# Narrowing the second half of the first expert's output weights in that expert's first two tiles

## The chip, the core and the metric

The kernel runs on one core of one Trainium2 chip. The metric is the device time of one execution in microseconds (us); of several executions the median counts.

## The reference

Four batches of talking-heads attention (12 heads, 448 positions, head size 64) are followed by two dense experts over 1792 tokens of width 768.

```python
scores = einsum(scale * q @ k.T, w_pre)          # mixes heads
attn = einsum(softmax(scores), w_post)           # mixes heads again
x = (attn @ v) laid out as 1792 x 768

h = x @ w_in                                     # first expert, 768 -> 1024
solu = h * softmax(h)
x = (normalised(solu) * g_ln) @ w_out            # 1024 -> 768

g = relu(x @ w2_in) ** 2                         # second expert, 768 -> 2048
out = g @ w2_out                                 # 2048 -> 768
```

The weights of both experts arrive as 64-bit words (the launch hands their arrays over as int64 views). The kernel has to make 32-bit floats of them itself; this is what "narrowing" means below.

## The kernel before, in words

The program's order is written by hand: each engine executes its instructions in the order in which the Python code emits them, and a function that yields lets the caller place its steps between other work.

**Attention.** The loop at line 624 goes over slots. A slot takes two blocks of ten query rows through the head mixing before the softmax (`pre`), row maxima (`negmax`, line 267), exponentials (`expo`, line 274), weights (`weigh`, line 285 and 287, once a slot), the head mixing after it (`post`, line 307) and the copy out of PSUM (`post_out`, line 337). Some slots also hold score matmuls (`qk`) or value matmuls (`av`, line 373). A last `x_out` (line 403) stores the attention's result as xD.

**Narrowing the first expert's weights** happens in the slots of the attention. `w1pieces` (line 413) lists pieces of 128 x 256 words: 24 of w_in, then 24 of w_out. `load_w1` (line 419) loads one through POOL's queue. `narrow` needs a square on ACT (line 82) and three operations on DVE (lines 85, 89, 93) that put the 32-bit word together; `flush` (lines 102 and 103) sets tiny numbers to zero in two operations on POOL; `scale_w1` (line 440) multiplies a piece of w_out by g_ln on ACT; `store_w1` (line 445) writes it back to HBM through SP's queue. Lines 618 to 645 pace the loads: `share` is the traffic of a slot if all pieces and the other loads are spread evenly over slots 5 to 63. The DVE steps are put in by `filler`, seven in each slot that has an `av` (line 675).

**First expert.** The loop at line 919 goes over 14 tiles `m` of 128 tokens. It loads and splits tile m + 2 into a high and a low part (`load_x`, `split_x`: ACT line 762, POOL line 763), runs the matmuls `h1` of tile m (line 500), then `norm1` (lines 773 to 794: the row maximum on DVE, exp on ACT, the product, statistics and their aggregate on DVE, rs on POOL, nb on DVE, the scaling on ACT), then `zt` of tile m - 1 (transposes on PE, line 809, a cast on ACT and a subtraction on DVE, line 812). The weights of w_out are loaded and split two blocks of 128 rows a tile in tiles 0 to 3 (`load_w1_out`, `split_w1_out`: ACT line 748, POOL line 749). From tile 4 on, two output matmul groups `out1` (line 823) stand in each tile.

**Narrowing the second expert's weights** is done by `w2stream` (line 844), which is stepped with `steps2`. A piece is loaded through SP (line 852), squared on ACT (line 862), made a mask on POOL (line 863: one operation), put together by three operations on DVE (lines 887, 891, 893) that take the mask in, and stored through SP (line 870). A load waits for the buffer of the piece five before it. `rate` says how many steps stand at each of four places in a tile:

```python
def rate(m, n):
    return 0 if m <= GT else n if m < NTILE - 1 else n // 2
...
steps2(rate(m, 4))
next(norm)
```

With GT = 3 no step stands in tiles 0 to 3; from tile 4 on there are 4 + 6 + 4 + 4 = 18 steps a tile. Sixty pieces go there, 36 later, in the second expert (line 1324), whose loop over 16 passes ends the program.

Of the kernel before, what the change touches and what calls it, by code (L numbers as in the profile page):

```python
# [11 lines left out]
AF = mybir.ActivationFunctionType  # L12
# [6 lines left out]
def kernel(  # L19
# [16 lines left out]
    nc = tc.nc  # L36
# [3 lines left out]
    NT, DM = out.shape  # L40
    F1 = w1_in.shape[1]
# [13 lines left out]
    scale = 1.0 / float(D) ** 0.5  # L55
# [7 lines left out]
    w1oD = dram.tile([F1, DM], F32, name="w1oD")  # L63
# [11 lines left out]
    g_sb = const.tile([128, F1 // 128], F32, name="g_sb")  # L75
# [64 lines left out]
    for b in range(B):  # L140
        for (i0, n) in CHUNKS:
# [10 lines left out]
            elif odd:  # L152
                k = nks[0] - 1
                order = [(1, k)] + order[:-2] + [(0, k)]
            for h, k in order:
                r = len(range(k, (n0, n - n0)[h], nks[h]))
# [9 lines left out]
    kk = {}  # L166
# [241 lines left out]
    WP = 256  # L408
# [2 lines left out]
    w1s = {}  # L411
    w1t = {}
    w1pieces = [(w1_in, w1iD, k, o) for k in range(CC) for o in range(0, F1, WP)]
    w1pieces += [(w1_out, w1oD, k, o) for k in range(F1 // 128) for o in range(0, DM, WP)]

    def load_w1(i):
        src, dst, k, o = w1pieces[i]
# [92 lines left out]
    def run(part):  # L510
        for _ in part:
            pass
# [215 lines left out]
    K1 = F1 // 128  # L728
# [16 lines left out]

    def split_w1_out(kk, r):
        t = m1_p.tile([128, 2, DM], F32R, name=f"w1o{kk}")
        nc.scalar.copy(t[:, 0], r)
        nc.gpsimd.tensor_tensor(out=t[:, 1], in0=r, in1=t[:, 0].bitcast(F32), op=ALU.subtract)  # L749
        w1o.append(t)  # L750
# [46 lines left out]
    GT = 3  # L797
# [37 lines left out]
    NE = F2 // FE  # L835
    KE = FE // 128
    FIRST = 60
    w2pieces = []
    for e in range(NE):
        w2pieces += [(w2_in, w2iD, c, e * FE) for c in range(CC)]  # L840
        w2pieces += [(w2_out, w2oD, e * KE + f, o) for f in range(KE) for o in range(0, DM, WP)]
    narrowed = []

    def w2stream(todo, nr, home):

        raws, ts, ready = {}, {}, []

        def load(i):
            if i in todo:
                src, dst, k, o = w2pieces[i]  # L850
                raws[i] = home(i, True)
                nc.sync.dma_start(out=raws[i], in_=src[k * 128:(k + 1) * 128, o:o + WP])

        def words(i):
            pair = raws[i].bitcast(U32).rearrange("p (n two) -> p n two", two=2)
            return pair[:, :, 0], pair[:, :, 1]

        def mask(i):

            if i in todo:  # L860
                t = ts[i] = home(i, False)
                nc.scalar.activation(out=t, in_=words(i)[1].bitcast(F32), func=AF.Square)  # L862
                nc.gpsimd.tensor_scalar(  # L863
                    out=t, in0=t, scalar1=2.0**-30, scalar2=2.0 - 2.0**-23, op0=ALU.is_ge, op1=ALU.mult
                )

        def store():
            i = ready.pop(0)
            src, dst, k, o = w2pieces[i]
            nc.sync.dma_start(out=dst[k * 128:(k + 1) * 128, o:o + WP], in_=ts.pop(i))  # L870
            narrowed.append(i)

        a = todo[0]
        for i in range(nr - 1):
            load(a + i)
        yield True
        mask(a)
        yield True
        mask(a + 1)
        yield True  # L880
        for i in todo:
            load(i + nr - 1)
            mask(i + 2)
            low, high = words(i)
            bits = ts[i].bitcast(U32)
            stt = nc.vector.scalar_tensor_tensor
            stt(out=bits, in0=high, scalar=3, in1=bits, op0=ALU.logical_shift_left, op1=ALU.bitwise_and)
            yield True
            if ready:
                store()  # L890
            stt(out=bits, in0=high, scalar=0xC0000000, in1=bits, op0=ALU.bitwise_and, op1=ALU.bitwise_or)
            yield True
            stt(out=bits, in0=low, scalar=29, in1=bits, op0=ALU.logical_shift_right, op1=ALU.bitwise_or)
            raws.pop(i)
            ready.append(i)
            yield True
        store()
        yield True
# [3 lines left out]
            return m1b_p.tile([128, WP], I64, tag="nraw", name="nraw", bufs=5)  # L902
        return m1b_p.tile([128, WP], F32, tag="nt", name="nt", bufs=5)

    stream = w2stream(range(FIRST), 5, home1)

    NTILE = NT // 128

    def rate(m, n):
        return 0 if m <= GT else n if m < NTILE - 1 else n // 2  # L910

    def steps2(n):
        for _ in range(n):
            next(stream, None)
# [2 lines left out]
    wr = {}  # L917
    outs = []
    for m in range(NTILE):
        if m + 2 < NTILE:  # L920
            xr[m + 2] = load_x(m + 2)
        if m:
            run(h1(m))
        norm = norm1(m)
# [3 lines that stand above are left out]
        if m > 0:  # L928
            zt(m - 1)
        if m <= GT:  # L930
            run(norm)
        steps2(rate(m, 6))
        if m + 2 < NTILE:
            split_x(m + 2, xr.pop(m + 2))
        for kk in range(len(w1o), min(K1, len(w1o) + 2)):
            wr[kk] = load_w1_out(kk)
        for kk in sorted(wr):
            split_w1_out(kk, wr.pop(kk))
        if m > GT and (m - 1) % GT == 0:
            outs += [((m - 1) // GT - 1, cc) for cc in range(CC)]  # L940
        for i in range(2):
            if outs:
                out1(*outs.pop(0))
            if i == 0:
                run(norm)
            steps2(rate(m, 4))
# [374 lines left out]
        t = wi2a_p.tile([128, HT], F32, tag=f"xb{i // 2 % 2}{i % 2}", name="nt", bufs=2)  # L1321
        return t[:, 0:WP]

    stream = w2stream(range(FIRST, len(w2pieces)), 4, home2)
    parts = []
    for q in range(NQ):
        p = q // NE
        work = plan(q)
        if q == NE - 1:
            parts = [((1, name), c) for name in ORDER for c in range(HC)]  # L1330
            load_xc(*parts[0][0])
            load_xc(*parts[HC][0])
        seq = SEQ_P if q < SW else SEQ
        for k, x in enumerate(seq):
            if isinstance(x, str):
                prod(q, x)
                after(q, x)
            elif q:
                y2(q - 1, x)
            lows()  # L1340
            for f, a in work.pop(k, []):
                f(*a)
            if parts:
                t, c = parts[0]
                if q == NE - 1 and (t[1] in ("p2", "p4") or t[1] in ("p7", "p3") and k < 7):
                    t = None
                if t:
                    parts.pop(0)
                    split_xc(*t, c)
                    i = ORDER.index(t[1]) + 2  # L1350
                    if c == HC - 1 and i < len(ORDER):
                        load_xc(1, ORDER[i])
            if q <= NE - 3:
                if q or k > 5:
                    steps2(2)
                if q == NE - 3 and k == len(seq) - 1:
                    run(stream)
                    next(mx)
            elif q == NE - 2 and k:
                next(mx, None)  # L1360
        assert not work
        if q < NE:
            assert len(narrowed) >= min(12 * (q + 2) + 6, len(w2pieces)), (q, len(narrowed))
    assert not parts
    for x in YO:
        y2(NQ - 1, x)
# [60 lines left out]
```

## Time and profile before

| what | us |
|---|---|
| median of three runs | 1088.48 |
| the runs | 1084.94 to 1094.23 |
| profiled execution, its own time | 1095.68 |
| its span in the profile | 1093.9 |

The profile is of one execution. Engines are named PE (matmuls), PEld (its weight loads), DVE, ACT, POOL and SP (which only issues DMAs). Lines are those of the kernel. In a row of instructions in order of time the columns are start and duration in us, engine, line, operation, tiles written and read, shapes and count, then in brackets the engine's idle time before it and what ended it.

### The profile page before, as it was taken

How to read it: one execution, taken by the hardware profiler on the slowest of the kernel's cores; microseconds unless marked ns; L12 is line 12 of the kernel's file. 1: busy time of each engine (PE TensorE's matmuls, PEld its weight loads, DVE VectorE, ACT ScalarE, POOL GpSimd, SP SyncE). 2: the span in 40 equal slices, each digit the busy share in tenths (PEclk: the TensorE clock that was granted, in tenths of full speed). 3: DMA queues.
4: the chain of work that ended last, by engine and by line, in shares of the span. 5: the costliest groups of instructions: out<-in, count | busy, mean ns of one | idle time of the engine just before them, and what ended most of it. 6: DMA issues, size and time to landing. Idle time of an engine off the chain costs nothing.

```text
span 1093.9 us, 30131 instructions
## 1 busy us (share of the span) xinstructions
PE 1036.3 (95%) x12220; PEld 888.7 (81%) x12220; DVE 681.7 (62%) x1131; ACT 563.0 (51%) x1195; POOL 672.2 (61%) x868
## 2 busy tenths in 40 slices
PE   7889879989899899999999999999999999999998
PEld 3565557656566588999989999999999999999998
DVE  2567858877676526889887525777656833444444
ACT  3666757777687535344344446344334655444432
POOL 4667978888674826656464258666536756666630
PEclk9999999999999999999999999999999999999999
DMA  7778787887865624665564746354455531111102
GB/s 230 189 203 250 233 232 217 259 257 238 245 189 179 196 56 130 189 204 169 178 192 128 240 127 199 121 157 159 157 190 193 184 108 58 59 59 58 58 29 101
DMA packets 115914, 181.06 MB, mean 166 GB/s; under 512 B 24224, under 2 KB 87200, under 8 KB 115776
## 3 DMA queue, kind: packets, MB, share of 16 engines
q1 hardware_dynamic: 100276, 127.79, 38.0%
q0 software_dynamic: 12608, 48.55, 14.8%
q10 hardware_dynamic: 2892, 2.80, 0.9%
q8 instruction: 96, 1.57, 0.6%
q14 instruction: 42, 0.34, 0.1%
HBM read 102.42 MB, written 38.14 MB: 128 GB/s over the span
## 4 chain that ended last, share of the span: by engine, by line
PE 55%; POOL 3%; issue 3%; DVE 1%; ACT 1%; DMA 1%; POOLq 0%; ACTq 0%
PE ps_y L1240 19%; PE ps_h L1169 17%; PE ps_o L823 10%; PE ps_h L500 7%; POOL ti L1097 1%; PE ps_tr L809 1%; POOL to L1105 1%; POOL s L1077 0%; DVE st L782 0%; DVE e L779 0%; DMA ra<-w2iD 0%; POOL w1o L749 0%; ACT e L776 0%; DMA xD<-xt 0%; POOL xs L763 0%
## 5 line engine op out<-in xcount | busy, mean ns | idle before, releaser
L1240 PE MATMUL ps_y<-to,gt 128*128 128x384 f32 x1332 | 241.8, 336 | 2.7 <-POOL to L1105 1.8
L1240 PEld LDWEIGHTS ps_y<-to,gt 128*128 128x128 f32 x1332 | 233.6, 188 | 5.0 <-POOL to L1105 2.1
L1169 PE MATMUL ps_h<-xc,ti 128*128 128x448 f32 x1080 | 225.1, 362 | 0.6 <-ACT h L1185 0.6
L1169 PEld LDWEIGHTS ps_h<-xc,ti 128*128 128x128 f32 x1080 | 201.6, 187 | 13.2 <-ACT h L1185 1.0
L337 DVE COPY at<-ps_ring 128x840 f32<-128x840 f32 (+2 forms) x114 | 96.0, 853 | 82.8 <-PE ps_ring L307 82.6
L307 PEld LDWEIGHTS ps_ring<-w,e 60*64 60x64 f32 x5040 | 92.4, 135 | 61.5 <-issue 34.3
L1251 DVE TENSOR_TENSOR y<-ps_y,y 128x768 f32<-128x768 f32 x97 | 92.4, 954 | 76.9 <-PE ps_y L1240 76.3
L863 POOL TENSOR_SCALAR nt<-nt 128x256 f32<-128x256 f32 x96 | 111.7, 1163 | 44.5 <-ACT nt L862 38.9
L307 PE MATMUL ps_ring<-w,e 60*64 60x60 f32 x5040 | 99.8, 221 | 31.2 <-issue 23.8
L274 ACT ACTIVATE e<-ps_pre,nm 128x448 f32<-128x448 f32 x180 | 112.9, 636 | 32.0 <-DVE nm L267 30.4
L267 DVE TENSOR_REDUCE nm<-ps_pre 128x1 f32<-128x448 f32 x180 | 104.0, 617 | 31.2 <-PE ps_pre L256 29.0
L229 ACT COPY ssrc<-ps_ring 128x896 f32<-128x896 f32 x92 | 83.3, 906 | 74.9 <-PE ps_ring L222 72.5
L823 PE MATMUL ps_o<-zt,w1o 128*128 128x384 f32 (+1 forms) x720 | 120.5, 326 | 0.2 <-POOL w1o L749 0.2
L500 PE MATMUL ps_h<-w1i,xs 128*128 128x512 f32 x504 | 119.7, 395 | 0.6 <-POOL xs L763 0.6
L823 PEld LDWEIGHTS ps_o<-zt,w1o 128*128 128x128 f32 x720 | 116.9, 189 | 0.7 <-POOL w1o L749 0.5
L500 PEld LDWEIGHTS ps_h<-w1i,xs 128*128 128x128 f32 x504 | 95.0, 190 | 20.8 <-POOL xs L763 1.5
L222 PE MATMUL ps_ring<-k,q 64*64 64x448 f32 x752 | 101.5, 564 | 10.8 <-issue 2.7
L1097 POOL TENSOR_TENSOR ti<-ra,ti 128x384 fp32r<-128x384 f32 x56 | 59.6, 1070 | 80.3 <-ACT ti L1096 79.7
L1182 DVE TENSOR_TENSOR gt<-h,gt 128x448 fp32r<-128x448 f32 x64 | 50.5, 789 | 90.2 <-ACT gt L1187 85.6
L862 ACT ACTIVATE nt<-nraw 128x256 f32<-128x256 f32 x96 | 41.0, 433 | 119.3 <-DMA w2iD<-nt 35.3
L256 PE MATMUL ps_pre<-sdst,wpre_bd 64*64 64x448 f32 (+1 forms) x720 | 96.0, 548 | 5.7 <-DMA sdst<-ssrc 2.3
L1105 POOL TENSOR_TENSOR to<-ro,to 128x768 fp32r<-128x768 f32 x32 | 61.2, 1918 | 46.1 <-ACT to L1104 45.6
(111 smaller groups left out, 1523.9 us busy)
## 6 DMA issues: line engine op xcount, KB each, us to landing
sdst<-ssrc SPq DMA_DIRECT2D x166, 210.0 KB
nraw<-in_moe_w_in_dram SPq DMA_DIRECT2D x48, 256.0 KB
nraw<-in_moe_w_out_dram SPq DMA_DIRECT2D x48, 256.0 KB
ra<-w2iD POOLq DMA_DIRECT2D x32, 384.0 KB, 4.4
ro<-w2oD POOLq DMA_DIRECT2D x32, 384.0 KB, 4.0
w1raw<-in_moe_w_in_dram POOLq DMA_DIRECT2D x24, 256.0 KB, 6.2
w1raw<-in_moe_w_out_dram POOLq DMA_DIRECT2D x24, 256.0 KB, 6.5
w2iD<-nt SPq DMA_DIRECT2D x48, 128.0 KB
```

Of the source, the lines that this page charges most:

```text
L222: nc.tensor.matmul(out=ps[64 * u:64 * u + 64, e, 0:S], lhsT=qq[c][64 * e:64 * e + 64, p * n + u * half:p * n + u * half + 64], rhs=k[64 * ...
L256: nc.tensor.matmul(out=ps[b][64 * u:64 * u + 64, 0:S], lhsT=wpre_bd[64 * r:64 * r + m], rhs=ds[b][64 * r:64 * r + m], start=True, stop=True,)
L267: nc.vector.tensor_reduce(out=nm, in_=pres[s][b][:, 0:S], op=ALU.max, axis=AX.X, negate=True)
L274: nc.scalar.activation(out=e, in_=pres[s][b][:, 0:S], func=AF.Exp, bias=nms.pop((s, b)), scale=1.0, accum_out=sms[s][:, b:b + 1])
L307: nc.tensor.matmul(out=ps[64 * c:64 * c + 64, u, i0:i0 + PR], lhsT=ee[b][64 * u:64 * u + m, o:o + 64], rhs=w[64 * u:64 * u + m, b], start= ...
L337: nc.vector.tensor_copy(dst[:, :, :, RH * k:RH * k + RH], pv[h, :, n0:n1])
L500: nc.tensor.matmul(out=ps[:, u], lhsT=t[:, a, cc], rhs=w1i[cc][:, w, u * 512:(u + 1) * 512], start=(cc == 0 and a == 0 and w == 0), stop=( ...
L823: nc.tensor.matmul(out=ps[:, 0:width], lhsT=w1o[k][:, w, cc * 128:(cc + 1) * 128], rhs=zT[:, a, k, 0:width], start=(k == 0 and i == 0), st ...
L863: nc.gpsimd.tensor_scalar(out=t, in0=t, scalar1=2.0**-30, scalar2=2.0 - 2.0**-23, op0=ALU.is_ge, op1=ALU.mult)
L1169: nc.tensor.matmul(out=bank[b][:, 0:HT], lhsT=t[:, w, c], rhs=xc[xn][:, a, c], start=(first and j == 0 and c == 0 and i == 0), stop=(j == ...
L1240: nc.tensor.matmul(out=ps[:, u - u2[0], 0:DM // 2], lhsT=gt[:, a, f, o:o + 128], rhs=w[:, v, f, u * (DM // 2):(u + 1) * (DM // 2)], start= ...
L1251: nc.vector.tensor_tensor(out=yo, in0=po, in1=yo, op=ALU.add)
```

## The change

Of the 24 pieces of w_out the last 12 (rows 512 to 1023) leave `w1pieces`. They stand at the front of `w2pieces` instead and are narrowed by `w2stream` in tiles 0 and 1 of the first expert, 18 steps in each, with the rest (`run(stream)`) at the head of tile 2, ahead of that tile's `load_x`. A second stream then takes the 60 pieces as before from tile 4 on. For the blocks 4 to 7 of w_out, the product with g_ln is now one operation on ACT over 128 x 768 in `split_w1_out`, in tiles 2 and 3.

```diff
-    w1pieces += [(w1_out, w1oD, k, o) for k in range(F1 // 128) for o in range(0, DM, WP)]
+    KL = F1 // 256
+    w1pieces += [(w1_out, w1oD, k, o) for k in range(KL) for o in range(0, DM, WP)]
...
     def split_w1_out(kk, r):
         t = m1_p.tile([128, 2, DM], F32R, name=f"w1o{kk}")
+        if kk >= KL:
+            nc.scalar.activation(out=r, in_=r, func=AF.Copy, scale=g_sb[:, kk:kk + 1])
         nc.scalar.copy(t[:, 0], r)
...
-    w2pieces = []
+    w2pieces = [(w1_out, w1oD, k, o) for k in range(KL, K1) for o in range(0, DM, WP)]
+    NL = len(w2pieces)
...
-    stream = w2stream(range(FIRST), 5, home1)
+    stream = w2stream(range(NL), 5, home1)
...
     def rate(m, n):
-        return 0 if m <= GT else n if m < NTILE - 1 else n // 2
+        return 0 if 1 < m <= GT else n if m < NTILE - 1 else n // 2
...
     for m in range(NTILE):
+        if m == 2:
+            run(stream)
+            stream = w2stream(range(NL, NL + FIRST), 5, home1)
...
-    stream = w2stream(range(FIRST, len(w2pieces)), 4, home2)
+    stream = w2stream(range(NL + FIRST, len(w2pieces)), 4, home2)
```

## Rows read from the trace of the kernel before

**Rows 1.** The chain that ended last, shares of the span by line.
```profile
PE ps_y L1240 19%; PE ps_h L1169 17%; PE ps_o L823 10%; PE ps_h L500 7%; POOL ti L1097 1%; PE ps_tr L809 1%; POOL to L1105 1%; POOL s L1077 0%; DVE st L782 0%; DVE e L779 0%; DMA ra<-w2iD 0%; POOL w1o L749 0%; ACT e L776 0%; DMA xD<-xt 0%; POOL xs L763 0%
```
**Rows 2.** Windows: length, busy PE, PEld, DVE, ACT, POOL; PEclk, DMA share, GB/s.
```profile
57.90:317.70 259.80, 229.03 (x5828) 156.70 (x5828) 188.91 (x349) 177.58 (x434) 207.71 (x367) 0.97 0.80 234
317.70:349.60 31.90, 30.09 (x834) 20.39 (x834) 19.56 (x34) 23.36 (x57) 14.65 (x31) 1.00 0.60 188
397.69:416.12 18.43, 17.73 (x82) 14.15 (x81) 10.25 (x18) 9.28 (x13) 7.48 (x8) 1.00 0.29 82
435.16:636.60 201.44, 201.23 (x1133) 187.45 (x1132) 151.88 (x297) 83.16 (x167) 109.37 (x101) 1.00 0.60 182
```
**Rows 3.** Instructions in order of time, PE: the first output matmuls.
```profile
435.16 4.26 PE L823 MATMUL ps_o<-zt,w1o 128*128 128x384 f32 x23
```
**Rows 4.** Instructions in order of time, DVE, tiles 0 to 2.
```profile
397.69 1.23 DVE L773 TENSOR_REDUCE nm<-ps_h 128x1 f32<-128x1024 f32 x1 [12.13 <-DMA xD<-xt]
...
403.27 0.21 DVE L784 BATCH_NORM_AGGREGATE mv<-st 128x2 f32<-128x12 f32 x1
404.41 0.16 DVE L790 SCALAR_TENSOR_TENSOR nb<-mv,rs 128x1 f32<-128x1 f32 x1 [0.93 <-POOL rs L787]
405.85 1.23 DVE L773 TENSOR_REDUCE nm<-ps_h 128x1 f32<-128x1024 f32 x1 [1.28 <-PE ps_h L500]
...
413.61 1.29 DVE L812 TENSOR_TENSOR zt<-ps_tr,zt 128x512 fp32r<-128x512 f32 x2
416.12 1.23 DVE L773 TENSOR_REDUCE nm<-ps_h 128x1 f32<-128x1024 f32 x1 [1.22 <-PE ps_h L500]
```
**Rows 5.** Windows of line 287 alone (once a slot): length, POOL busy (count).
```profile
57.90:317.70 259.80, 24.96 (x62) 0.97 0.80 234
317.70:349.60 31.90, 3.48 (x9) 1.00 0.60 188
...
225.10:259.10 34.00, 3.63 (x9) 1.00 0.84 246
```
**Rows 6.** Waits of PE from 58 to 318 us: total us, times, longest.
```profile
PE ps_ring L307 <- issue: 19.1, 11, 3.7
PE ps_ring L222 <- issue: 2.7, 3, 1.5
PE ps_pre L256 <- issue: 2.3, 1, 2.3
```
**Rows 7.** Windows in which the granted clock was low; columns as in rows 2.
```profile
62.10:65.50 3.40, 3.40 (x34) 2.00 (x28) 3.26 (x9) 1.67 (x4) 1.14 (x3) 0.50 0.89 197
...
287.40:290.80 3.40, 2.90 (x43) 1.86 (x47) 1.15 (x2) 1.79 (x7) 2.11 (x5) 0.50 0.88 277
```
**Rows 8.** Groups by line, narrowing in the attention: count, busy us, mean ns.
```profile
L102 POOL TENSOR_SCALAR w1sq<-w1sq 128x256 f32<-128x256 f32 x48 | 41.0, 854 | 4.9 <-ACT w1sq L82 0.9
L103 POOL TENSOR_TENSOR w1t<-w1t,w1sq 128x256 f32<-128x256 f32 x48 | 35.3, 734 | 4.0
L89 DVE SCALAR_TENSOR_TENSOR w1t<-w1raw,w1t 128x256 uint32<-128x256 uint32 x48 | 21.1, 440 | 1.4
L419 POOL DMA_DIRECT2D w1raw<-in_moe_w_out_dram x24 | 14.3, 595 | 1.0 <-DVE w1t L85 0.9
L440 ACT ACTIVATE w1t<-w1t,g_sb 128x256 f32<-128x256 f32 x24 | 10.8, 509 | 0.0
```
**Rows 9.** Instructions in order of time, DVE, tile 4: operations of the narrowing.
```profile
447.87 0.42 DVE L891 SCALAR_TENSOR_TENSOR nt<-nraw,nt 128x256 uint32<-128x256 uint32 x1
448.33 1.95 DVE L893 SCALAR_TENSOR_TENSOR nt<-nraw,nt 128x256 uint32<-128x256 uint32 x1
```
**Rows 10.** Instructions in order of time, POOL, the same stretch of tile 4.
```profile
442.94 4.95 POOL L863 TENSOR_SCALAR nt<-nt 128x256 f32<-128x256 f32 x4 [0.52 <-ACT nt L862]
447.97 2.02 POOL L763 TENSOR_TENSOR xs<-xraw,xs 128x768 fp32r<-128x768 f32 x1
```
**Rows 11.** Instructions in order of time, POOL, tile 0.
```profile
408.45 3.66 POOL L749 TENSOR_TENSOR w1o<-w1oraw,w1o 128x768 fp32r<-128x768 f32 x2
```

More of the change, by code (lines that the diff above doesn't have):

```diff
@@ L1362 @@
         if q < NE:
-            assert len(narrowed) >= min(12 * (q + 2) + 6, len(w2pieces)), (q, len(narrowed))
+            assert len(narrowed) >= min(NL + 12 * (q + 2) + 6, len(w2pieces)), (q, len(narrowed))
     assert not parts
```

## The prediction

> **What bounds the kernel now.** I read the chain of waits first. Of the span, 19% is matmuls of the second expert's output, 17% of its input, 10% and 7% those of the first expert [rows 1]: from about 440 us on, TensorE's own work is the path. The page's chain does not reach back into the attention, so there I read windows, slots and waits.
>
> Then the windows by stage. From 435.16 to 636.60 us PE is busy 201.23 of 201.44 us [rows 2]: whatever delays the first output matmul (435.16, line 823) moves everything behind it one for one [rows 3]. Between the first and the third row maximum of the first expert (397.69 and 416.12) DVE works 10.25 of 18.43 us [rows 2, 4]. That is the stage which receives the work: tiles 0 and 1 have no output matmuls, so PE has little more to do there than h1 and the transposes, and about 8.2 us of DVE time are free.
>
> For the stage that gives the work I compare slots. Line 287 runs once a slot: 62 slots from 57.9 to 317.7 us, 4.19 us each, with the narrowing; 9 slots from 317.7 to 349.6, 3.54 us each, without it [rows 5]. The reader is to see also which wait is behind the difference: in the narrowing stretch PE waits 19.1 + 2.7 + 2.3 = 24.1 us for "issue", nothing that the profile shows [rows 6], with the DMA engines 80% busy against 60% later [rows 2]. After four of these gaps the granted clock stood at 0.50 for some 3.4 us (first and last in [rows 7]), the lower level of 1.2 GHz: about 1.7 us lost each time, 6.8 us together. So of 62 x 0.65 = 40 us that these slots cost beyond the others, some 31 are stalls, of a kind that the slots with less traffic don't have.
>
> **What the change takes from the attention.** Twelve of 48 pieces. Each had on DVE three operations of 0.44 us or less (lines 85 to 93), on POOL 0.854 + 0.734 us of flush and 0.595 us of issuing its load, on ACT a square and a scaling of 0.509 us, on SP a store [rows 8]. That is at most 15.8 us of DVE, 26.2 us of POOL and 12 x 384 KB = 4.7 MB, 8% of what 234 GB/s moves in 259.8 us. None of it is lone on the path. The pacing at lines 618 to 642 spreads the 36 pieces that are left over the same slots, so none of the stage simply ends earlier: the 144 steps fed by the filler become 108, with 1 to 5 fewer in most slots that hold an `av`.
>
> What that gives back, from both sides. A low end: the nine slots from 225.1 to 259.1 narrow as well and take 34.0 us against 31.9 for the nine without [rows 5]; 2.1/9 x 62 = 14.5 us for all pieces, a quarter is 3.6. A plain quarter of the 40 is 10. A high end: if traffic falls from 80% to some 74% and stalls halve, 15.5 + 2 (a quarter of the other 9) = 18. I take 8, near the plain quarter and a little under it, because k, v and q loads are in these slots too and stay. Scores and values themselves are untouched.
>
> **What it adds to tiles 0 and 1.** 36 narrowing operations on DVE, 12 masks on POOL, 12 squares on ACT, 12 loads and 12 stores on SP; the masks no longer need the second flush operation. The order is written by hand, so I follow DVE's queue with rows of the same operations. One follows the other at 0.45 us (447.87 to 448.33) [rows 9], a mask takes 4.95/4 = 1.24 us [rows 10].
>
> Tile 0. The aggregate ends at 403.48, POOL's rs just before 404.41 [rows 4]. The first narrowing operation now stands before nb and waits for the first mask, which is behind rs: 404.4 + 1.24 + 0.42, then nb 0.16, gives 406.2 for nb's end, 1.6 us late. Fourteen more operations stand before the next row maximum: 14 x 0.45 = 6.3. A stop belongs to them: the operation at 448.33 took 1.95 us instead of 0.42, from inside POOL's xs subtraction (447.97, 2.02 us) to its end [rows 9, 10]; a hold costs 1.5 us. In tiles 0 and 1 POOL has three such subtractions each (xs, and two w1o of 1.83 us [rows 11]). Behind five masks, xs and the first w1o reach DVE's narrowing: two holds, 3.0. The second row maximum starts at 406.2 + 6.3 + 3.0 = 415.5 instead of 405.85.
>
> Tile 1. Maximum to aggregate takes 5.8 us, as in tile 0 (397.69 to 403.48): 421.3. Four operations, 1.8; nb and the zt subtractions, 0.16 + 1.29 [rows 4]: 424.5. Fourteen more, 6.3, with two holds, 3.0: 433.8. The twelfth piece runs at the head of tile 2: its mask stands on POOL behind both w1o subtractions, 1.24 of waiting, and three operations, 1.35. The third row maximum starts at 436.4 instead of 416.12: 20 us late.
>
> From there to the output matmuls nothing shortens: the transposes of tile 2, h1 of tile 4 and the transposes of tile 3 still follow one another on PE, 19.0 us before (416.12 to 435.16) [rows 3, 4]. The four scalings of 128x768 on ACT, in tiles 2 and 3, are not in the trace; by 0.509 us for a third of the width [rows 8] each is 0.5 to 1.5, I take 0.85, and they lie in ACT's waits for DVE. SP's queue now has the loads of w1o behind raw loads that wait for DVE, and the x tile of tile 4 behind the last store; both arrive before DVE is ready for what needs them, and if not, the price is POOL's 1.9 us each. PE stands idle some 8 us before tile 2's transposes. A fall of the clock after that costs 1.7 us; I count 1.
>
> Bounds of this term: if all 8.2 us of DVE's free time are filled and nothing is held, 16.2 - 8.2 = 8; if all six subtractions hold for their whole length, 16.2 + 6 x 1.85 + 2.5 = 30 with no free time used. I take 20 + 1, since little of the free time can be used: the waits for exp stand before the first narrowing operation in program order.
>
> The Trainium skill (SBUF — State Buffer, section "SBUF: two separate sides") says that VectorE and GpSimd share a port pair under an exclusive lock, kept for a whole instruction, and that a VectorE operation with two SBUF inputs takes part in it against any GpSimd operation that reads SBUF. The held operation agrees with it (1.95 us); the one at 447.87 does not, since it took 0.42 us while a mask, which reads SBUF, was running [rows 9, 10].
>
> **Sum.** +20 +1 -8 = +13 us. The profiled execution took 1095.68 us (span 1093.9), 7.2 above the median of 1088.48; its own time becomes 1108.7. The 13 us are set against the median: 1101.5.
>
> **Rivals.**
> 1. The stalls halve: the attention gives 18, the tiles cost 21; about +3, 1091.5. For: waits without a shown cause stand only where traffic is at 0.80. Against: 8% fewer bytes is little.
> 2. The attention gives nothing, because PE's own queue bounds its slots: +21, 1109.5. For: the nine slots at 34.0. Against: the mean of all slots.
> 3. DVE's free time hides more than I grant, term 8 instead of 20: about 0, 1088. For: 8.2 us idle. Against: the hand-written order.
> 4. Masks hold DVE as well: twelve more holds of 1.24 - 0.42 = 0.8 us, terms 30 + 1 - 8, +23, 1111.5. Against: the rows 9 operation at 447.87. The rule of the Trainium skill cited above would give this.
> 5. The other side: the issue stalls come from the narrowing's loads and go almost wholly once traffic drops under the level at which they occur. Price 31 + 2 = 33 gained against 21: -12, 1076.5. It decides once more than some 19 us of the 24.1 + 6.8 vanish. For: after 317.7 no such wait is left. Against: a quarter of the loads goes, not all, and k, v, q stay.
> That the pieces are not moved at all is excluded by the lists of pieces.
>
> **Chances.** My forecast with its spread (+7 to +18) 0.50, rival 1 0.15, rival 2 0.15, rival 3 0.08, rival 4 0.05, rival 5 0.07. One per cent, 10.9 us, is about what a measurement of this kernel can tell from no change. Of the forecast's 0.50 some 0.38 lies above it; with rivals 2 and 4 that is 0.58 slower. The other 0.12 with rivals 1 and 3 makes 0.35 within; rival 5 is 0.07 faster. The range 1087 to 1112 leaves out rival 5 and the far tails of 2 to 4, near 0.2; the forecast's own is 1095 to 1107.
>
> **What would show it.** Right: in the changed profile the second and third row maxima start about 9.6 and 20 us later after the first than now, with the narrowing between; the first output matmul follows the first maximum by 57 us instead of 37.5; the first maximum comes about 8 us earlier; PE has a gap near 8 us before tile 2's transposes. Wrong: first-to-third distance under 30 us (rival 3) or over 45 (rival 4), a first maximum earlier by 15 or more with issue waits halved (rivals 1, 5) or unmoved (rival 2); or a narrowing DVE operation held by masks.

## The result and the profile after

| | before | after |
|---|---|---|
| median of six runs each, us | 1087.35 | 1104.19 |
| the runs, us | 1083.95 to 1094.23 | 1099.68 to 1106.42 |
| profiled execution, its own time, us | 1095.68 | 1099.68 |
| its span, us | 1093.9 | 1097.9 |

The ratio is 1.0117, 95% interval 1.0082 to 1.0151: slower, by 12.7 us at its middle (8.9 to 16.4), where 13 were forecast. The medians of the table stand 16.8 us apart, a little more than the interval's upper end; a repeat (experiment 5) has the ratio 1.0127 and medians 11.5 us apart. Gains and losses in us below are the ratio's, times the median of the kernel before. The two traces differ by 4 us alone, because the one of before is slower than all six of its runs and the one of after is the fastest of its six. A difference of two traces must therefore be split into a part that repeats and a part that doesn't before anything is read from it.

**The receiving stage.** The lines of the first expert stand 1 to 4 further down in the kernel after. DVE in order of time, tiles 0 and 1 and the head of tile 2, after (it answers to [rows 4]):
```profile
377.89 1.22 DVE L776 TENSOR_REDUCE nm<-ps_h 128x1 f32<-128x1024 f32 x1 [12.10 <-DMA xD<-xt]
...
383.47 0.21 DVE L787 BATCH_NORM_AGGREGATE mv<-st 128x2 f32<-128x12 f32 x1
385.79 0.43 DVE L891 SCALAR_TENSOR_TENSOR nt<-nraw,nt 128x256 uint32<-128x256 uint32 x1 [2.11 <-POOL nt L867]
386.13 0.35 DVE L793 SCALAR_TENSOR_TENSOR nb<-mv,rs 128x1 f32<-128x1 f32 x1
...
389.04 0.50 DVE L895 SCALAR_TENSOR_TENSOR nt<-nraw,nt 128x256 uint32<-128x256 uint32 x1
...
391.81 1.91 DVE L895 SCALAR_TENSOR_TENSOR nt<-nraw,nt 128x256 uint32<-128x256 uint32 x1
393.76 0.42 DVE L897 SCALAR_TENSOR_TENSOR nt<-nraw,nt 128x256 uint32<-128x256 uint32 x1
394.10 1.22 DVE L776 TENSOR_REDUCE nm<-ps_h 128x1 f32<-128x1024 f32 x1
...
407.98 1.92 DVE L895 SCALAR_TENSOR_TENSOR nt<-nraw,nt 128x256 uint32<-128x256 uint32 x1
...
416.31 0.43 DVE L891 SCALAR_TENSOR_TENSOR nt<-nraw,nt 128x256 uint32<-128x256 uint32 x1 [4.69 <-POOL nt L867]
...
417.57 1.22 DVE L776 TENSOR_REDUCE nm<-ps_h 128x1 f32<-128x1024 f32 x1
```
Follow the row maxima. The second one had a wait in front of it before, for h1 on PE; now it starts where the last narrowing operation ends, with no bracket: DVE's own queue is late, not PE. First to second maximum is 16.21 us (8.16 before), first to third 39.68 (18.44 before). One narrowing operation a tile is held: it takes 1.91 or 1.92 us. The last piece waits 4.69 us for its mask.

POOL in the same stretch, after, shows who holds and who makes it wait (answers to [rows 10, 11]):
```profile
384.67 6.65 POOL L867 TENSOR_SCALAR nt<-nt 128x256 f32<-128x256 f32 x5
391.40 2.04 POOL L766 TENSOR_TENSOR xs<-xraw,xs 128x768 fp32r<-128x768 f32 x1
395.00 3.66 POOL L752 TENSOR_TENSOR w1o<-w1oraw,w1o 128x768 fp32r<-128x768 f32 x2 [1.56 <-ACT w1o L751]
...
407.62 2.00 POOL L766 TENSOR_TENSOR xs<-xraw,xs 128x768 fp32r<-128x768 f32 x1
411.18 3.93 POOL L752 TENSOR_TENSOR w1o<-w1oraw,w1o 128x768 fp32r<-128x768 f32 x2 [1.57 <-ACT w1o L751]
415.20 1.07 POOL L867 TENSOR_SCALAR nt<-nt 128x256 f32<-128x256 f32 x1
```
The held operations end 0.28 us after the xs subtractions (393.44 and 409.62). While the five masks of tile 0 run, twelve narrowing operations take 0.41 to 0.50 us each (389.04 is one of them): masks hold nothing. The two w1o subtractions start at 395.00, when tile 0's narrowing is over, and in tile 1 at 411.18, when only the last piece is left; no narrowing operation is held by them (one starts 0.01 us after the subtraction at 411.18 and takes 0.42 us), but that piece's mask stands behind them. ACT tells why they are late. The casts in front of them, after:
```profile
394.09 0.83 ACT L751 CAST w1o<-w1oraw 128x768 fp32r<-128x768 f32 x1 [4.89 <-DMA w1oraw<-w1oD]
...
396.65 1.10 ACT L779 ACTIVATE e<-ps_h,nm 128x1024 f32<-128x1024 f32 x1
...
410.27 0.83 ACT L751 CAST w1o<-w1oraw 128x768 fp32r<-128x768 f32 x1 [3.46 <-DMA w1oraw<-w1oD]
```
ACT waits 4.89 and 3.46 us for the weights, and what stands behind the casts waits with it: tile 1's exp at 396.65 starts 1.3 us after its row maximum is there (394.10 + 1.22). SP's queue in order of time, after, has the issue of these loads behind a raw load of the narrowing:
```profile
388.68 0.33 SPq L856 DMA_DIRECT2D nraw<-in_moe_w_out_dram  x1
389.05 0.90 SPq L744 DMA_DIRECT2D w1oraw<-w1oD  x2
```
and what the raw loads wait for there, from 377 to 420 us:
```profile
SPq L856 <- DVE nt L897: 16.5, 4, 7.5
```
A raw load waits for the buffer of the piece five before, that is, for DVE, and the weights' loads wait behind it. They are issued from 389.05 on, when ACT is 0.15 us from needing them, and the first is there 5.0 us later.

PE, after (answers to [rows 3]):
```profile
393.49 9.05 PE L501 MATMUL ps_h<-w1i,xs 128*128 128x512 f32 x32 [2.67 <-POOL xs L766]
...
425.79 1.97 PE L812 MATMUL ps_tr<-id_sb,e 128*128 128x128 f32 x8 [6.64 <-ACT e L797]
427.40 10.04 PE L501 MATMUL ps_h<-w1i,xs 128*128 128x512 f32 x36
...
438.07 4.26 PE L826 MATMUL ps_o<-zt,w1o 128*128 128x384 f32 x23
```
The first output matmul follows the first maximum by 60.18 us (37.47 before): the stage became 22.7 us longer.

**The giving stage.** Windows of after: slots 9 to 71, slots 72 to 80, first to third maximum, and 201 us from the first output matmul; columns as in [rows 2], to which they answer:
```profile
54.80:299.90 245.10, 225.33 (x5829) 154.21 (x5829) 174.82 (x314) 169.25 (x412) 181.76 (x332) 0.99 0.79 233
299.90:332.10 32.20, 30.08 (x836) 20.73 (x836) 19.54 (x33) 22.82 (x55) 14.01 (x31) 1.00 0.59 178
377.90:417.57 39.67, 30.86 (x118) 23.37 (x117) 27.95 (x55) 14.63 (x26) 27.87 (x22) 0.83 0.53 161
438.07:639.00 200.93, 200.02 (x1124) 186.14 (x1123) 150.70 (x297) 84.99 (x169) 109.22 (x99) 1.00 0.59 180
```
In this pair the narrowing slots are 14.7 us shorter, and the nine behind them are as long as before (32.2 and 31.9). The first row maximum comes 19.8 us earlier (377.89 instead of 397.69). In the third window PEclk is 0.83, where before it was 1.00: two stretches of 6.8 us at 0.50 stand in it behind gaps of PE, and a third begins at 424.0, in the gap ahead of tile 2's transposes. From the first output matmul on, nothing has changed. Waits of PE over the same slots, after (answers to [rows 6]; total us, times, longest):
```profile
PE ps_ring L307 <- issue: 8.5, 9, 3.6
PE ps_ring L222 <- issue: 3.3, 3, 1.2
PE ps_ring L373 <- issue: 2.7, 3, 1.3
```
14.5 us of "issue" instead of 24.1. Whether that is the change or the execution, one pair can't say: in the four traces whose attention is that of the kernel after (its two, experiments 1 and 3) these waits are 12.5 to 21.0 us.

### The profile page after: what moved, and what is told of

The parts are those of the page before. It is cut to its first block, busy times and chain, and to the rows that moved or that the text cites. A ratio compares the mean times of both kernels' runs of the same rounds, so it can differ in the third digit from the quotient of the medians.

```text
span 1097.9 us, 30100 instructions
## 1 busy us (share of the span) xinstructions
PE 1040.5 (95%) x12220; PEld 889.6 (81%) x12220; DVE 682.8 (62%) x1131; ACT 562.4 (51%) x1187; POOL 661.7 (60%) x844
## 4 chain that ended last, share of the span: by engine, by line
PE 49%; POOL 5%; DVE 4%; issue 3%; DMA 3%; ACT 2%; SPq 0%; POOLq 0%; ACTq 0%; DVEq 0%
PE ps_y L1247 19%; PE ps_h L1176 16%; PE ps_o L826 8%; PE ps_h L501 6%; POOL ti L1104 1%; POOL nt L867 1%; DMA ra<-w2iD 1%; POOL w1o L752 1%; POOL s L1084 1%; DVE st L785 1%; DMA w2oD<-nt 1%; DVE e L782 1%; POOL to L1112 1%; PE ps_tr L812 1%; DVE nt L891 0%
## 5 line engine op out<-in xcount | busy, mean ns | idle before, releaser
L867 POOL TENSOR_SCALAR nt<-nt 128x256 f32<-128x256 f32 x108 | 126.3, 1170 | 43.0 <-ACT nt L866 31.8
L501 PE MATMUL ps_h<-w1i,xs 128*128 128x512 f32 x504 | 124.4, 406 | 5.2 <-POOL xs L766 3.4
L501 PEld LDWEIGHTS ps_h<-w1i,xs 128*128 128x128 f32 x504 | 98.1, 197 | 27.4 <-POOL xs L766 4.9
L866 ACT ACTIVATE nt<-nraw 128x256 f32<-128x256 f32 x108 | 45.7, 433 | 115.9 <-DMA w2iD<-nt 38.4
```

The costliest lines, as they stand in the source:

```text
L501: nc.tensor.matmul(out=ps[:, u], lhsT=t[:, a, cc], rhs=w1i[cc][:, w, u * 512:(u + 1) * 512], start=(cc == 0 and a == 0 and w == 0), stop=( ...
L867: nc.gpsimd.tensor_scalar(out=t, in0=t, scalar1=2.0**-30, scalar2=2.0 - 2.0**-23, op0=ALU.is_ge, op1=ALU.mult)
```

## The experiments

What had to be told apart: whether the two terms (attention -8, tiles +21) are what they were forecast to be, since +13 could also be +5 with nothing gained; and what in the twelve pieces the attention pays for.

**1. The giving stage alone.** The kernel before without the twelve pieces, and nothing put in their place.
```diff
-    w1pieces += [(w1_out, w1oD, k, o) for k in range(F1 // 128) for o in range(0, DM, WP)]
+    w1pieces += [(w1_out, w1oD, k, o) for k in range(F1 // 256) for o in range(0, DM, WP)]
...
-        nc.sync.dma_start(out=r, in_=w1oD[kk * 128:(kk + 1) * 128, :])
+        k = kk % (K1 // 2)
+        nc.sync.dma_start(out=r, in_=w1oD[k * 128:(k + 1) * 128, :])
```


> The kernel before without the last 12 pieces: they are narrowed nowhere, and blocks 4 to 7 of the output weights are read from blocks 0 to 3 (so that much work is left out). Attention alone changes. My theory: the attention gives back about 8 us (between 4 and 18), so about 1079 against 1087, with PE's waits for issue and the low-clock stretches fewer, and the 37.5 us from first row maximum to first output matmul unchanged. Rival (the attention gives nothing): 1087. Rival (stalls go almost wholly): 1055 to 1065.

Measured: 1083.22 against 1092.51 on the same chip, ratio 0.9926 (0.9896 to 0.9956): 8.1 us gained (4.8 to 11.4). The tile stage is untouched to the hundredth: maxima 8.16 and 18.44 us after the first, output matmul at +37.47. So -8 stands, and the rivals in which the attention gives 0, 18 or 33 fall.

**2. The receiving stage alone.** All 48 pieces stay in the attention, and twelve are narrowed once more in tiles 0 and 1.
```diff
+    w2pieces = [(w1_out, w1xD, k, o) for k in range(KL, K1) for o in range(0, DM, WP)]
+    NL = len(w2pieces)
...
-        return 0 if m <= GT else n if m < NTILE - 1 else n // 2
+        return 0 if 1 < m <= GT else n if m < NTILE - 1 else n // 2
```


> The kernel before with all 48 pieces narrowed in the attention, and the last 12 narrowed a second time in tiles 0 and 1 into a spare buffer that nobody reads (blocks 4 to 7 are scaled a second time, to have the same operations). Tiles alone change. My theory: +21 us, from 20 to 23, so about 1109; the third row maximum comes 39 to 40 us after the first. Rival (DVE's free time hides it): +8 or less. If this and the run without the 12 pieces add up to the change's own +13 to +17, the two terms are independent.

Measured: 1113.92, ratio 1.0205 (1.0159 to 1.0250): 22.4 us lost. The trace has the maxima at +16.20 and +40.31, the output matmul at +60.30, as the kernel after has them. The loss's interval is 17.4 to 27.3 us. The two halves add up to 22.4 - 8.1 = 14.3; the change itself gave 12.7, and 13.9 when it was run again in experiment 5. Within these intervals of 4 to 5 us to either side the terms add up, and each can be read by itself.

**3. The last mask's wait.** The kernel after, with nine steps ahead of tile 1's split instead of six, and one at its end instead of four. The mask of the last piece then goes ahead of the subtractions.
```diff
-        steps2(rate(m, 6))
+        steps2(9 if m == 1 else rate(m, 6))
...
-            steps2(rate(m, 4))
+            steps2((4, 1)[i] if m == 1 else rate(m, 4))
```


> The changed kernel with 9 instead of 6 steps ahead of tile 1's split and 1 instead of 4 at its end: the twelfth piece's mask stands on POOL ahead of tile 1's three subtractions instead of behind them. If DVE's 4.69 us wait at the head of tile 2 is that queue's doing: the wait goes, the third row maximum comes 3 to 4.5 us sooner, and the time falls by as much, to about 1100 from 1104. Rival (PE's transposes, xs or the clock decide there): the wait moves elsewhere, and the time stays within 1 us.

Measured: 1100.53, ratio to before 1.0108 (1.0066 to 1.0150), not to be told from the kernel after. The trace shows what became of the wait. DVE in order of time, end of tile 1:
```profile
414.16 0.43 DVE L891 SCALAR_TENSOR_TENSOR nt<-nraw,nt 128x256 uint32<-128x256 uint32 x1 [0.43 <-POOL nt L867]
414.62 1.92 DVE L895 SCALAR_TENSOR_TENSOR nt<-nraw,nt 128x256 uint32<-128x256 uint32 x1
416.58 1.94 DVE L897 SCALAR_TENSOR_TENSOR nt<-nraw,nt 128x256 uint32<-128x256 uint32 x1
418.44 1.21 DVE L776 TENSOR_REDUCE nm<-ps_h 128x1 f32<-128x1024 f32 x1
```
4.69 us of waiting became 0.43, and two operations of the last piece are now held, where one operation of the tile was. POOL in the same stretch names the holders:
```profile
414.21 2.06 POOL L766 TENSOR_TENSOR xs<-xraw,xs 128x768 fp32r<-128x768 f32 x1
416.23 3.98 POOL L752 TENSOR_TENSOR w1o<-w1oraw,w1o 128x768 fp32r<-128x768 f32 x2
```
The third maximum comes at +36.66 instead of +39.68, the output matmul at +56.59 instead of +60.18. Moving the wait gives back 3.6 us of 22.7 (2.3 against the repeat of the kernel after, which has +58.93); most of the rest is the operations themselves and the holds.

**4. Traffic without engine work.** The kernel before, with the twelve pieces loaded and their raw words stored, and no operation on DVE, ACT or POOL in between.
```diff
+    idle = [(w1_out, w1oD, k, o) for k in range(F1 // 256, F1 // 128) for o in range(0, DM, WP)]
...
+        if w1pieces[i] in idle:
+            t = w1raw.pop(i).bitcast(F32)
+            nc.sync.dma_start(out=dst[k * 128:(k + 1) * 128, o:o + WP], in_=t[:, 0:WP])
+            return
```


> As the run without the last 12 pieces, but their loads and stores stay, one after every three narrowed pieces: the raw words' first half is stored as it came, no square, narrowing, flush or scaling. So traffic as before, engine work as without them. If the attention's gain comes from traffic (PE's waits for issue): about as slow as before, 1084 to 1088. If it comes from the engines' work (DVE, POOL, ACT in the slots with value matmuls): as fast as the run without the pieces, about 1079.

Measured: 1087.83, ratio 0.9952 (0.9915 to 0.9989), a gain of 5.2 us (1.2 to 9.3). It lies between the two theories and decides nothing by itself; but it is clear of zero, with all the loads and stores still there.

**5. Engine work without traffic, and the change again.** The other way round: no load and no store for the twelve, while all their operations run on the raw words of the piece before.
```diff
+        if w1pieces[i] in idle:
+            w1raw[i] = w1kept[i - 1]
+            return
...
+        if w1pieces[i] in idle:
+            w1t.pop(i)
+            return
```


> The counterpart of the run with traffic alone: no loads and no stores for the last 12 pieces, but their engine work stays, on the raw words of the piece before (every third piece is narrowed, flushed and scaled twice, the second result goes nowhere; blocks 4 to 7 are read from 0 to 3). If engine work is what the attention gives back: as slow as before, 0.998 to 1.000. If traffic (the waits for issue) is: about 0.993, as without the pieces. In between means that both carry a part.

Measured: 1079.48 against 1091.62, ratio 0.9890 (0.9853 to 0.9927), a gain of 12.0 us (8.0 to 16.0). With the whole engine work in place the kernel gains at least as much as without any of the twelve's work (0.9926). So the loads and stores carry the gain, or the larger part of it. What the engines' work costs stays open: leaving it out gave 5.2 us in experiment 4, where the loads and stores stay, and nothing where they are gone (8.1 gained without it in experiment 1, 12.0 with it here). PE's waits over slots 9 to 71 of this kernel, the longest:
```profile
PE ps_ring L307 <- issue: 4.4, 4, 1.8
```
The kernel after once more, on the same chip:

> The changed kernel once more, on the chip of the runs beside it. 1.012 times the kernel before (1.008 to 1.015), with 60.2 us from the first row maximum to the first output matmul; that distance has no noise worth speaking of, the attention has some 10 us of it.

Measured: 1103.13, ratio 1.0127 (1.0087 to 1.0167). The first output matmul follows the first maximum by 58.93 us, 1.25 less than was expected, and the third maximum stands at +38.98. DVE at the end of tile 1 has the reason:
```profile
410.21 1.96 DVE L897 SCALAR_TENSOR_TENSOR nt<-nraw,nt 128x256 uint32<-128x256 uint32 x1
415.07 0.43 DVE L891 SCALAR_TENSOR_TENSOR nt<-nraw,nt 128x256 uint32<-128x256 uint32 x1 [2.89 <-POOL nt L867]
```
The weights of tile 1 came 3.03 us late for ACT here (3.46 in the first trace, 4.47 in experiment 2). So the first w1o subtraction, at 409.76, did meet a narrowing operation and held it, and the last mask was waited for 2.89 us (4.69 and 5.46 in the other two).

**6. More traffic, first try.** The kernel before with twelve additional loads, each stored raw.
```diff
+    idle = [(w1_in, w1xD, k, o) for k in range(3) for o in range(0, F1, WP)]
+    w1pieces = [p for i in range(len(idle)) for p in w1pieces[4 * i:4 * i + 4] + idle[i:i + 1]]
```


> The kernel before with twelve further loads of 256 KB through POOL's queue and twelve stores of 128 KB in the attention, one pair after every four pieces, into a buffer that nobody reads; no engine work is added, and nothing is left out. If traffic is what a piece costs in the attention: +8 to +12 us, 1.007 to 1.011 of the kernel before. If engine work is: within 3 us of it.

Measured: 1113.15 against 1091.67, ratio 1.0206 (1.0169 to 1.0243), far more than either theory. Waits of POOL's engine and queue from 58 to 336 us, first row:
```profile
POOL w1raw L423 <- DMA w1xD<-w1raw: 25.9, 6, 6.7
```
and of PE:
```profile
PE ps_ring L308 <- POOL w L288: 20.0, 16, 4.0
```
The raw buffer is stored directly, so POOL's next load into it waits until that store has landed; POOL stands still with the weights of the slot (line 288) behind the load, and PE waits for them. So the kernel measured a held queue, and what part traffic has in it can't be told. (Experiment 4 stores raw words too, but POOL has no such wait in its trace.) The run is told because the mistake is easily made: a DMA that waited for a buffer here stopped everything behind it on the engine that issued it.

**7. More traffic, with less of a hold.** Two kernels. One has 24 more loads into a single buffer of their own that nobody reads; the other stores every narrowed piece a second time. Each adds 6.3 MB and no engine work.
```diff
+        if i % 2:
+            t = raw_p.tile([128, WP], I64, tag="w1two", name="w1two", bufs=1)
+            nc.gpsimd.dma_start(out=t, in_=src[k * 128:(k + 1) * 128, o:o + WP])
```
```diff
-        nc.sync.dma_start(out=dst[k * 128:(k + 1) * 128, o:o + WP], in_=w1t.pop(i))
+        nc.sync.dma_start(out=dst[k * 128:(k + 1) * 128, o:o + WP], in_=w1t[i])
+        nc.sync.dma_start(out=w1xD[k * 128:(k + 1) * 128, o:o + WP], in_=w1t.pop(i))
```


> The kernel before, with 24 more loads of 128x256 words (6.3 MB) through POOL's queue beside every second load of the narrowing, into a buffer of their own that nothing reads; no engine work and no store is added, and what is computed is the kernel's. Traffic theory (the pieces cost the attention what their bytes cost): the 12 pieces that e1_relief takes out moved 4.7 MB and gave 8 us, so 6.3 MB more cost 10.7 us, ratio 1.010. If only stores cost (the stall theory with DMA writes to HBM as cause): 1.000. If it is the engines' work or PE's own queue: 1.000. If it is POOL's issuing, 24 times 0.6 us = 14 us of POOL's time, which was never the bound in the attention: 1.000 to 1.003.

> The kernel before, with every narrowed piece stored a second time, to another place in HBM that nothing reads: 48 more stores of 128x256 floats (6.3 MB, as many bytes as in e10_loads) through SP's queue; no load and no engine work is added, and what is computed is the kernel's. Traffic theory: again 10.7 us, ratio 1.010. If only loads cost: 1.000. The two together tell whether the price goes with bytes of either kind.

Measured, against 1094.65 on the same chip: loads 1108.54, ratio 1.0133 (1.0098 to 1.0167), 14.6 us; stores 1107.85, ratio 1.0118 (1.0079 to 1.0158), 12.9 us. More of either kind costs, some 2.1 to 2.3 us a MB; the twelve pieces' 4.7 MB gave 8.1 in experiment 1 and 12.0 in experiment 5, that is 1.7 and 2.5 us a MB. In the tiles both kernels are as before (output matmul at +37.48 and +37.47). The windows of slots 9 to 71, first of the kernel with engine work and no traffic for the twelve (experiment 5):
```profile
54.53:293.69 239.16, 224.03 (x5828) 151.79 (x5828) 189.41 (x349) 177.11 (x434) 200.98 (x356) 1.00 0.81 237
```
of the kernel with more loads:
```profile
58.74:328.56 269.82, 232.49 (x5828) 158.65 (x5827) 190.55 (x349) 178.05 (x434) 217.16 (x387) 0.97 0.85 246
```
and of the kernel with more stores:
```profile
57.79:327.57 269.78, 237.29 (x5829) 161.46 (x5829) 189.48 (x349) 177.60 (x434) 207.80 (x369) 0.98 0.82 243
```
GB/s times length gives the bytes: 56.7, 66.4 and 65.6 MB in 239, 270 and 270 us; the kernel before has 60.8 MB in 259.8 [rows 2], the one after 57.1 MB in 245.1. DVE's and ACT's work is the same in the first, the last two and the kernel before. The rate hardly moves in these five (233 to 246 GB/s), the length goes with the bytes. Single executions scatter around that (in the trace of experiment 1, 56.9 MB took 250.8 us), so the price is taken from the ratios. And DMA share is no measure of it: with 0.81 the first is the fastest of all.

The price of the loads is not of bytes alone. A load into the one buffer waits for the load before it, and so the hold of experiment 6 is here too, if smaller; POOL and PE of the kernel with more loads, from 58 to 318 us:
```profile
POOL w1two L423 <- DMA w1two<-in_moe_w_in_dram: 7.5, 3, 5.1
PE ps_ring L307 <- POOL w L287: 6.3, 2, 4.6
```
POOL waited 4.9 us more for such loads of w_out. Of the 14.6 us some 6 can be this hold.

Where PE waits is another matter. With more stores, from 58 to 318 us:
```profile
PE ps_ring L308 <- issue: 11.1, 8, 2.3
PE ps_pre L257 <- DMA sdst<-ssrc: 8.8, 8, 2.5
```
"Issue" is lower than in the kernel before, and the shuffled scores now arrive late instead (line 257). Their DMAs stand in SP's queue, where the further stores stand too. So it is shown that more loads and more stores cost, and that fewer gain; but not that the bytes alone set the price, apart from the places that they take in POOL's and SP's queues, nor that it is paid through issue waits.

**8. Another place for the pieces.** Between the last copy out of PSUM and the first row maximum DVE is idle 12.10 us, as the first row of after above shows. The stream was put there, with buffers of its own, for the last six, nine or all twelve pieces. The edit for nine, against the kernel after:
```diff
-    KL = F1 // 256
+    KL = F1 // 128 - 3
     w1pieces += [(w1_out, w1oD, k, o) for k in range(KL) for o in range(0, DM, WP)]
...
+        if s == NP:
...
+            run(w2stream(range(NL), 9, home0))
```


> Blocks 5 to 7 of the output weights (nine pieces instead of twelve) leave the attention's slots; they are narrowed where DVE, ACT and POOL idle, between the last copy out of the head mixing and the first row maximum, with nine buffers of their own and nothing in tiles 0 and 1. If the tiles' cost is DVE's queue between the row maxima: the 37.5 us from first maximum to first output matmul stay within 1 us, the first maximum waits at most 2 us for the narrowing, and the attention gives 3/4 of its 8: about 0.995 of the kernel before (0.990 to 0.999). Rival (the squares ahead of the last value matmuls hold ACT's copies, and with them the last store of xD): the first maximum comes 4 us or more later, and the time is as before or above.

> The same with blocks 6 and 7 only (six pieces): the first maximum does not wait at all, and the attention gives half of its 8: about 0.996 of the kernel before (0.992 to 1.000). Rival as for the nine pieces, with 2 us instead of 4.

> As the version with nine pieces in the idle time ahead of the first row maximum, but with all twelve: nine buffers for the raw words, so the last three loads wait for DVE, and their squares stand on ACT ahead of the last copies of the value matmuls. The attention's slots give back the whole 8 us or more; the first row maximum waits some 4 us for the last pieces: about 0.995 of the kernel before (0.991 to 1.000), no better than nine. Rival (ACT is free again in time, and DVE's 12 us of idle time hold twelve pieces as they hold nine): 0.991.

Measured: nine pieces 1084.35 against 1091.62, ratio 0.9957 (0.9921 to 0.9993); six 1089.31, 0.9972 (0.9944 to 1.0000); twelve 1087.23 against 1091.67, 0.9957 (0.9932 to 0.9981). Nine and twelve are faster than the kernel before by 4.7 us at the middle, under one per cent but clear of zero, and so faster than the one after, with all pieces narrowed; for six a gain is not shown, as its interval reaches 1. DVE of the kernel with nine, end of the idle time:
```profile
380.72 0.42 DVE L642 SCALAR_TENSOR_TENSOR nt<-nraw,nt 128x256 uint32<-128x256 uint32 x1
381.07 1.22 DVE L854 TENSOR_REDUCE nm<-ps_h 128x1 f32<-128x1024 f32 x1
```
The nine pieces' 27 operations fill the gap to its end: the second maximum comes 7.81 us after the first instead of 8.16, so the first was 0.35 late, and the output matmul is at +37.51. With twelve the distances are 6.91 and +38.42: the first is at least 1.25 late, the output matmul another 0.95 behind that, and so some 2.2 us of what the attention gives are spent again.

## Why the prediction was right

It held: 12.7 us at the middle of the interval for a forecast of 13, on the slower side, and each of the two large terms measured by itself (+22.4, -8.1) is near what was forecast (+21, -8). That the sum comes within 1 us is partly luck: these intervals are wider than that, and inside the tiles' term two errors cancel. By its own steps:

**Attention, -8.** Experiment 1 gave 8.1. Taking the value near a plain quarter of the slots' excess was right. The prediction put the gain down to fewer stalls. Experiment 5 shows that the loads and stores carry it, or the larger part of it; that it comes as fewer issue waits is not shown, since 24.1 and 14.5 us are two single executions, and with more stores another wait took their place. Rival 1 (halved stalls, 18 gained) and rival 5 (they go wholly) are out, since a quarter of the pieces gave 8.1 of the 40 us, near a quarter; so is rival 2 (nothing gained). The prediction's own sign for rivals 1 and 5, a first maximum earlier by 15 or more with issue waits halved, would have misled: in the pair of traces it comes 19.8 us earlier. But the trace of before was 8.3 us slower than its median run and the one of after 4.5 us faster, and without these 12.8 us some 7 are left.

**Tiles, +20.** The third maximum is 21.2 us later (39.68 against 18.44), so the term is 6% short, and two sizes in it were wrong in opposite directions. The step "two holds, 3.0" in each of the two tiles failed in the first trace: there was one hold a tile, 1.5 each, because the w1o subtractions came after the narrowing and not into it; that is 3 us less. The step "its mask stands on POOL behind both w1o subtractions, 1.24 of waiting" failed: it waited 4.69, 3.4 us more. Both have one cause, which the prediction had in its hands and left out of the sum: "SP's queue now has the loads of w1o behind raw loads that wait for DVE". It took them to arrive before they were needed; they came 4.89 and 3.46 us late for ACT, and POOL's subtractions with them. Three traces bear it out: the later the weights of tile 1 (3.03, 3.46, 4.47 us), the longer the wait for the last mask (2.89, 4.69, 5.46) and the later the third maximum (+38.98, +39.68, +40.31), and where they were least late the second hold of tile 1 was there. No run moved these loads alone ahead in SP's queue. The rest, 0.6 us, has the same root in its larger part: tile 1's exp, behind the late cast on ACT, made DVE wait 2.55 us instead of the 1.33 taken over from tile 0 (in tile 1 of before, where casts stood ahead of the exp as well, it was 2.10), and the 36 operations took some 0.6 us less than forecast. Experiment 3 shows the same from the other side: with the mask early, the wait falls to 0.43 us and the second hold appears.

**Masks.** Rival 4 (masks hold DVE too) is out by the rows from 384.67 to 391.32. The prediction's own row did not show it: the masks of [rows 10] end at 442.94 + 4.95 = 447.89, 0.02 us after the operation at 447.87 began. The rule of the Trainium skill (SBUF — State Buffer, "SBUF: two separate sides"), by which a VectorE operation with two SBUF inputs shares the lock with any GpSimd operation that reads SBUF, is borne out here for the subtractions (1.91 and 1.92 us against 0.42) and not for the masks.

**Rival 3**, that DVE's free time hides part of the work, is out by the windows: from first to third maximum DVE is busy 27.95 of 39.67 us instead of 10.25 of 18.43, so its idle time rose, from 8.2 to 11.7 us. Nothing was hidden, net; experiment 2 says the same with 22.4 us lost.

**Clock and PE, +1.** PE stood idle 6.64 us ahead of tile 2's transposes (8 forecast), and the granted clock fell as expected: the h1 matmuls behind it took 10.04 us for 36 (8.76 before) at a clock that was partly 0.50. Third maximum to output matmul is 20.50 us instead of 19.04, so 1.5 was paid. In tiles 0 and 1 PEclk fell as well; no row maximum waited for PE there, since DVE was late.

**The scaling on ACT** of 128 x 768, taken as 0.85 us, took 0.93 to 0.94. The step "they lie in ACT's waits for DVE" failed: two scalings stand ahead of tile 3's exp, and DVE waits for it, after:
```profile
431.00 0.15 DVE L780 TENSOR_SCALAR sm<-sm 128x1 f32<-128x1 f32 x1 [4.21 <-ACT e L779]
```
The wait was 1.33 us before, and the exp starts 12.2 us after the third maximum instead of 10.4. So not all of the 1.5 us need be the clock: in experiment 3's trace, where the granted clock was 1.00 from 421.8 us on, 0.9 us were paid, and PE waited 0.63 us for POOL's xs and, ahead of tile 3's transposes, 0.68 us for ACT.

## What to carry to other kernels

Work that is moved out of a crowded stage gains what the scarce thing there gains (here loads and stores more than engine time). Where it lands it can cost its full duration on the engine that sets the end, as it did here, whatever that engine's share of idle time is: idle time helps only if it stands, in program order, where the work is put. Look for such a stretch by the bracket ahead of an instruction; the 12 us ahead of the first row maximum took nine of the pieces for 0.35 us. And when a queue's DMAs wait for buffers, price whatever stands behind them in that queue, not only the bytes.

## What the runs showed of the hardware

Executions of one kernel differ by 10 us and more (1083.95 to 1094.23 in six runs of before), and in the traces the attention holds most of it: the four whose attention is that of the kernel after (the two of it, experiments 1 and 3) took 244.2 to 250.8 us for slots 9 to 71, but 659.8 to 661.1 us from the first output matmul to the end. First maximum to output matmul repeats to 0.02 us in the seven traces whose tiles are left alone (37.47 to 37.49), and to 1.3 us in the kernel after (60.18 and 58.93). A stage whose length repeats can be judged from one trace; the attention can't.

To the operations held by subtractions (1.91 to 1.96 us instead of 0.42) there is a counterpart: the masks are not waited for, but take longer beside narrowing operations, 6.65 us for five and 5.14 for four, against 2.23 for two and 1.07 for one alone (in the trace of after).

The unexplained "issue" gaps of PE have a companion. One row of the page's DMA queues in the kernel after (packets, MB, share of 16 engines):
```profile
q8 instruction: 96, 1.57, 0.6%
```
These are packets of 16 KB. From 40 to 300 us the fourteen traces of the kernels here have 106 PE gaps of more than 1 us without a shown releaser. Of them 101 end 1 to 2 us after such a packet has landed (half of them 1.39 to 1.54 us after), though one lands only every 5.6 us or so; packets shifted in time at random would give 19. That suits a PE that waits for its own instructions. If their packets came later the more loads and stores stand beside them, it would tie the traffic's price to these gaps. No run here changed the instruction packets alone, so it stays a suspicion, if a strong one.
